# Start-up of an attention and gated-MLP kernel: all of k loaded first, the squares of k and q on two engines, norm columns earlier, and own banks for the half-width first weight products

## The chip, the cores and the metric

The kernel runs on one core of a Trainium2 chip. The metric is the device time of one execution in microseconds (us), as a median of several executions. TensorE (PE) does the matmuls, VectorE (DVE) and ScalarE (ACT) the elementwise work, GpSimd (POOL) issues the loads, SyncE (SP) the stores and the transposing loads of v. The profile is of one execution and covers a span some 1.9 us shorter than the device time. Its granted clock is the share of the full TensorE clock that PE was given.

## The reference, cut to what matters

```python
# q, k, v: (4, 6016, 256) float32; tau = 1
qn = q / (norm(q, axis=1) + 1e-6)        # norms run over the 6016 rows
kn = k / (norm(k, axis=1) + 1e-6)
s = kn.transpose(0, 2, 1) @ qn / tau     # 256 x 256 per batch
a = softmax(s, axis=-1)
x = (v @ a).reshape(24064, 256)
g = x @ w_gate                           # 256 x 1536
out = (g * sigmoid(g) * (x @ w_val)) @ w_out
```

The kernel never forms x. For each batch it multiplies the softmax matrix into both weights, once, and then multiplies v by these products. The work of batches 1 to 3 ahead of their weights runs in the background of the batch before. Batch 0 has no such cover: its loads, norms, softmax and first weight products are the start-up, and only that is changed here.

## The kernel before

The norms of batch 0 are sums of squares. An engine squares a pair of 128-row slices into `sq`; PE adds the rows up with a matrix of ones. For q the last group of slices (three of them; the other groups have four) goes straight into columns, since q's norm is wanted per partition:

```python
def first_last_q(b, ts):
    sqs = [first_square(b, t, 0, on_dve=(t == NP - 1)) for t in ts]
    row = work.tile([1, C], FP32, tag="row")
    nc.vector.tensor_copy(row, state[b, "ss", 0][0:1, :])
    for t in ts:
        gemm1_pair(b, t)
    cols = psum_gv.tile([P, CH], FP32, tag="g")
    for h in range(CH):
        nc.tensor.matmul(cols[:, h:h + 1], row[0:1, h * P:(h + 1) * P], ones_f[0:1, 0:1], ...)
    for t, sq in zip(ts, sqs):
        ...                                  # column sums of the last squares
```

Loads and squares: k three groups ahead of q; all of k's squares on VectorE, all of q's but the last pair on ScalarE.

```python
K_AHEAD = 3
for g in range(NG + K_AHEAD):
    if g < NG: order.append((g, 1))          # k
    if g >= K_AHEAD: order.append((g - K_AHEAD, 0))   # q
for n, (g, which) in enumerate(order):
    load_qk(0, g, which)
    ...
load_first_v(); load_w(0); load_v(*allc[1]); load_w(1); load_w(2)
# then w_out
```

The first weight products ("units": unit 0 and 1 are w_gate, 2 and 3 w_val, each for one half of the output rows) are made in two half widths. The lower half is all that the first two gate and value products want. Both halves share one buffer of the accumulation memory (PSUM), called a bank in what follows; to evacuate it is to copy the result out, scaled:

```python
units = [psum_gv.tile([P, WP], FP32, tag="gv"[u % 2]) for u in range(4)]
...                                          # lower halves of units 0 to 3
for u in range(4):
    wp_evacuate(b, u, units[u], lo)          # even units ScalarE, odd ones VectorE
nc.scalar.preload_act_table(ACT.Silu)
for u in range(4):
    for jh in range(CH):
        wp_matmul(b, u, jh, units[u], hi)
    wp_evacuate(b, u, units[u], hi, on_dve=True)
```

Then step f = 0 to 11 of chunk 0: a gate and a value product (`g_ps`, `v_ps`), Silu on ScalarE, the multiplication on VectorE (`sv`), and two more units in full width as long as there are any.

## Time and profile before

| | kernel before |
|---|---|
| device time, median | 821.44 us |
| span of the profile | 819.5 us |
| PE busy | 804.1 us, 98% |
| last q tile landed | 34.26 us |
| root of the norm columns begins | 36.63 us |
| units 2 and 3 (w_val) begin | 38.71 us |
| first gate product begins | 40.67 us |

The last four lines date the start-up's hand-overs, in us from the start of the span. The landing is from the trace's landing records; the others are start times in the timeline. The root is ScalarE's square root of the norm columns. From 39.65 us to the end PE has next to no gaps (3.0 us in all, in six places), so an earlier first gate product with the same work behind it is an earlier end.

### The profile page before, as it was taken

The page shows a single profiled execution, that of the slowest core. Times are in us where ns is not written, and L with a number is a line of the kernel's source. Part 1 is how long each engine was busy: PE and PEld are TensorE (multiplying, and loading weights), DVE is VectorE, ACT ScalarE, POOL GpSimd, SP SyncE. Part 2 cuts the span into 40 slices and gives each one's busy share as a digit, 9 for nine tenths or more (in the row PEclk, how much of TensorE's full clock was granted, in tenths as well). Part 3 has the DMA queues.
Part 4 walks back from the last instruction along what each step waited for, and adds up shares of the span by engine and source line. Part 5 has one row for each costly group of instructions (what it writes and reads, how often), then busy time and mean ns, then how long its engine had stood idle before and what let it go on. Part 6 is the DMA issues. An engine that isn't in the chain of part 4 may idle for free.

```text
span 819.5 us, 13681 instructions
## 1 busy us (share of the span) xinstructions
PE 804.1 (98%) x5039; PEld 488.2 (60%) x5039; DVE 552.9 (67%) x882; ACT 462.1 (56%) x826; POOL 104.7 (13%) x204
## 2 busy tenths in 40 slices
PE   7799999999999999999999999999999999999998
PEld 4556556665565655666565655666656566566666
DVE  5577888667655888856755688875856555555554
ACT  2566677545555777745555676755454544544543
POOL 5533000114310000121330000011300000000000
PEclk9999999999999999999999999999999999999999
DMA  9999812227992121123997111232562112112101
GB/s 87 145 154 139 138 40 65 52 65 114 149 153 46 55 50 40 52 52 88 143 142 126 41 52 39 40 78 64 119 118 65 46 40 65 52 39 66 49 26 59
DMA packets 92675, 64.59 MB, mean 79 GB/s; under 512 B 52560, under 2 KB 91472, under 8 KB 91856
## 3 DMA queue, kind: packets, MB, share of 16 engines
q0 software_dynamic: 18656, 27.01, 26.0%
q1 hardware_dynamic: 73952, 36.71, 18.3%
q8 instruction: 39, 0.64, 0.3%
q14 instruction: 28, 0.23, 0.1%
HBM read 78.64 MB, written 36.70 MB: 141 GB/s over the span
## 4 chain that ended last, share of the span: by engine, by line
PE 92%; DMA 2%; DVE 2%; ACT 2%; issue 1%; POOL 1%; DVEq 0%; ACTq 0%; POOLq 0%
PE o_new L456 29%; PE v_ps L428 29%; PE g_ps L428 29%; DMA q_sb<-in_q_dram 2%; PE ps L397 2%; PE kq_new L149 2%; DVE sv L432 1%; ACT sq L274 1%; DVE acc_new L283 1%; POOL k_sb L104 0%; PE ss_new L176 0%; ACT sq L166 0%; ACT silu L431 0%; PE unit_ps L397 0%; POOL q_sb L104 0%
## 5 line engine op out<-in xcount | busy, mean ns | idle before, releaser
L432 DVE TENSOR_TENSOR sv<-silu,v_ps 128x512 bf16<-128x512 bf16 (+1 forms) x576 | 382.6, 673 | 219.3 <-ACT silu L431 217.8
L431 ACT ACTIVATE silu<-g_ps 128x512 bf16<-128x512 f32 (+1 forms) x576 | 337.5, 587 | 302.0 <-PE g_ps L428 282.1
L456 PE MATMUL o_new<-w_out_sb,sv 128*128 128x256 bf16 x2256 | 338.4, 273 | 0.0
L428 PE MATMUL v_ps<-vT,Wv 128*128 128x512 bf16 (+1 forms) x1128 | 330.4, 374 | 3.0 <-DVE sv L432 3.0
L428 PE MATMUL g_ps<-vT,Wg 128*128 128x512 bf16 (+1 forms) x1128 | 331.1, 375 | 0.0
L456 PEld LDWEIGHTS <-sv 128*128 128x128 bf16 x2256 | 220.7, 98 | 140.8
L428 PEld LDWEIGHTS <-Wv 128*128 128x128 bf16 x1152 | 112.7, 98 | 135.0 <-issue 5.3
L428 PEld LDWEIGHTS <-Wg 128*128 128x128 bf16 x1152 | 106.8, 98 | 27.2 <-issue 0.2
L283 DVE TENSOR_TENSOR acc_new<-acc_new,sq 128x512 f32<-128x512 f32 x135 | 93.2, 691 | 22.1 <-ACT sq L274 19.6
L274 ACT ACTIVATE sq<-q_sb 128x512 bf16<-128x512 fp8e5 x72 | 44.3, 615 | 0.0
L274 ACT ACTIVATE sq<-k_sb 128x512 bf16<-128x512 fp8e5 x72 | 44.1, 612 | 0.0
L149 PE MATMUL kq_new<-k_sb,q_sb 128*128 128x512 fp8e5 x184 | 43.4, 318 | 0.3 <-DMA q_sb<-in_q_dram 0.3
L292 POOL CAST hi<-acc_new 128x512 bf16<-128x512 f32 x3 | 1.8, 605 | 294.3 <-DVE acc_new L283 294.3
L465 ACT COPY o_sb<-o_new 128x512 f32<-128x512 f32 x48 | 28.1, 585 | 13.6 <-PE o_new L456 12.9
L467 DVE COPY o_sb<-o_new 128x512 f32<-128x512 f32 (+1 forms) x48 | 31.7, 661 | 3.0 <-PE o_new L456 3.0
L104 POOL DMA_DIRECT2D k_sb<-in_k_dram x48 | 25.9, 542 | 38.5 <-DMA q_sb<-in_q_dram 17.7
L104 POOL DMA_DIRECT2D q_sb<-in_q_dram x48 | 26.2, 546 | 33.2 <-DMA vb<-in_v_dram 9.8
L112 POOL DMA_DIRECT2D vb<-in_v_dram x47 | 23.8, 509 | 21.2 <-DMA k_sb<-in_k_dram 16.8
L176 PE MATMUL ss_new<-sq,ones_bf 128*128 128x256 bf16 x91 | 18.6, 293 | 6.5 <-DVE sq L163 5.1
L163 DVE TENSOR_TENSOR sq<-k_sb 128x512 bf16<-128x512 fp8e5 (+1 forms) x24 | 15.3, 681 | 13.8 <-DMA k_sb<-in_k_dram 13.7
L149 PEld LDWEIGHTS <-q_sb 128*128 128x256 fp8e5 x184 | 23.1, 140 | 2.0 <-DMA q_sb<-in_q_dram 0.8
L166 ACT ACTIVATE sq<-q_sb 128x512 bf16<-128x512 fp8e5 x23 | 13.0, 619 | 19.7 <-DMA q_sb<-in_q_dram 11.9
(92 smaller groups left out, 184.9 us busy)
## 6 DMA issues: line engine op xcount, KB each, us to landing
out_dram<-o_sb SPq DMA_DIRECT2D x92, 256.0 KB, 2.4
vb<-in_v_dram POOLq DMA_DIRECT2D x43, 256.0 KB, 9.6
k_sb<-in_k_dram POOLq DMA_DIRECT2D x44, 128.0 KB, 11.4
q_sb<-in_q_dram POOLq DMA_DIRECT2D x44, 128.0 KB, 11.4
w_gate_sb<-in_moe_w_gate_dram POOLq DMA_DIRECT2D x3, 256.0 KB, 9.5
w_val_sb<-in_moe_w_val_dram POOLq DMA_DIRECT2D x3, 256.0 KB, 9.6
w_out_sb<-in_moe_w_out_dram POOLq DMA_DIRECT2D x1, 768.0 KB, 14.3
vb<-in_v_dram POOLq DMA_DIRECT2D x4, 192.0 KB, 3.4
```

The costliest lines, as they stand in the source:

```text
L104: nc.gpsimd.dma_start(out=dst[:, gs:gs + gm, :], in_=src[b].rearrange("(p s) c -> p s c", s=NS)[:, gs:gs + gm, :])
L112: nc.gpsimd.dma_start(out=vb[:mv, :].rearrange("(p s) c -> p (s c)", s=cm), in_=v[b, cs * P:cs * P + mv, :].rearrange("(p s) c -> p (s c)" ...
L149: nc.tensor.matmul(kq[:, jh, :], q_sb[:, ps:ps + 2, js], k_sb[:, ps:ps + 2, :], start=(t == 0 and jh == 0), stop=last, perf_mode=DR, skip_ ...
L176: nc.tensor.matmul(state[b, "ss", which], ones_bf, sq[:, s, :], start=(t == 0 and s == 0), stop=(t == t_last and s == pm - 1))
L274: nc.scalar.activation(sq[:, :pm, which, :], qk_tiles[b][which][:, ps:ps + pm, :], ACT.Square)
L283: nc.vector.tensor_add(acc, acc, sq[:, s, :, :])
L428: nc.tensor.matmul(dst[:, :mv], W[:, kk, fs], vT[:, kk, :mv], start=(kk == 0), stop=(kk == CH - 1))
L431: nc.scalar.activation(silu[:, :mv], g_ps[:, :mv], ACT.Silu)
L432: nc.vector.tensor_mul(sv[:, f, :mv], silu[:, :mv], v_ps[:, :mv])
L456: nc.tensor.matmul(self.o_ps[:, j % 2, :], self.sv[:, f, j * P:(j + 1) * P], w_out_sb[:, f, :], start=(f == 0), stop=(f == FH - 1))
L465: nc.scalar.copy(o_sb[:, :m, :], self.o_ps[:, :m, :])
L467: nc.vector.tensor_copy(o_sb[:, :m, :], self.o_ps[:, :m, :])
```

## The change

Its intent: get k's norm out of the way before q is done, keep either engine from falling behind with q's squares, leave next to nothing between the last q tile and the root, and take the wait for the evacuations out of the first weight products by giving their upper halves banks of their own (from the pool `psum_o`). The core of the diff:

```diff
-    K_AHEAD = 3
-    order = []
...
+    order = [(g, 1) for g in range(NG)] + [(g, 0) for g in range(NG)]
...
-    keep_warm(10)
-    T_COLS = groups[NG - 1][0] // 2
+    G_COLS = NG - 3
+    T_COLS = groups[G_COLS][0] // 2
     for g, which in order:
...
+        if which == 0 and g == G_COLS:
+            first_row_copy(0)
+        sqs = [first_square(0, t, which, on_dve=(t % 2 == 1)) for t in ts]
+        if which == 0:
+            for t in ts:
                 gemm1_pair(0, t)
+            if g == G_COLS:
+                first_cols(0)
...                                # k's norm at q group 0, its reciprocals in four
...                                # pieces of 64 columns at q groups 1 to 4
-            unit_ps = psum_gv.tile([P, WP], FP32, tag="gv"[u % 2])
+            unit_ps = psum_gv.tile([P, HW], FP32, tag="gv"[u % 2])
...
         for u in range(4):
-            wp_evacuate(b, u, units[u], lo)
+            wp_evacuate(b, u, units[u], lo, u % 2 == 1)
+        for u in range(2):
+            wp_unit(b, u, psum_o, "o", hi)
         nc.scalar.preload_act_table(ACT.Silu)
-        for u in range(4):
-            for jh in range(CH):
-                wp_matmul(b, u, jh, units[u], hi)
-            wp_evacuate(b, u, units[u], hi, on_dve=True)
...
+            g_ps, v_ps, mv = gv_matmuls(b, ci, f)
+            us = range(2 * f + 2, min(2 * f + 4, len(wp_units))) if gi == 0 else ()
+            part = hi if f == 0 else full
+            for u in us[:1]:
+                wp_unit(0, u, psum_o, "o", part, on_dve=True)
+            silu = gv_silu(g_ps, mv)
+            for u in us[1:]:
+                wp_unit(0, u, psum_o, "o", part, on_dve=(f == 0))
+            gv_product(f, sv, silu, v_ps, mv)
```

The number of matmuls for the weights is the same; the upper halves of units 2 and 3 move behind the first gate and value products.

More of the change, by code (lines that the diff above doesn't have):

```diff
@@ L177, in first_row_sums, with first_row_copy, first_cols @@
                              start=(t == 0 and s == 0), stop=(t == t_last and s == pm - 1))
-    def first_last_q(b, ts):
-        sqs = [first_square(b, t, 0, on_dve=(t == NP - 1)) for t in ts]
+    def first_row_copy(b):
         row = work.tile([1, C], FP32, tag="row")
         nc.vector.tensor_copy(row, state[b, "ss", 0][0:1, :])
-        for t in ts:
-            gemm1_pair(b, t)
+        state[b, "row"] = row
+    def first_cols(b):
+        row = state[b, "row"]
         cols = psum_gv.tile([P, CH], FP32, tag="g")
@@ L190, in first_last_q, with first_col_sums @@
                              skip_group_check=True)
-        for t, sq in zip(ts, sqs):
-            pm = pairs[t][1]
-            for s in range(pm):
-                for h in range(CH):
-                    nc.tensor.matmul(cols[:, h:h + 1], sq[:, s, h * P:(h + 1) * P],
-                                     ones_bf[:, 0:1], start=False,
-                                     stop=(t == ts[-1] and s == pm - 1),
-                                     skip_group_check=True)
-        state[b, "cols"] = cols
+        state[b, "cols"] = cols
+    def first_col_sums(b, t, sq):
+        cols = state[b, "cols"]
+        pm = pairs[t][1]
+        for s in range(pm):
+            for h in range(CH):
+                nc.tensor.matmul(cols[:, h:h + 1], sq[:, s, h * P:(h + 1) * P],
+                                 ones_bf[:, 0:1], start=False,
+                                 stop=(t == NP - 1 and s == pm - 1),
+                                 skip_group_check=True)
     def first_root(dst, src):
@@ L209, in first_norm_k, with first_inv_k @@
         state[b, "ink"] = ink
-    def first_inv_k(b, h):
-        part = state[b, "ink"][:, h * P:(h + 1) * P]
+    def first_inv_k(b, n):
+        part = state[b, "ink"][:, n * (C // 4):(n + 1) * (C // 4)]
         nc.vector.reciprocal(part, part)
@@ L235, in first_softmax @@
                                  scale=inq[:, jh:jh + 1])
-        units = []
-        for u in range(2 * CH):
-            unit_ps = psum_gv.tile([P, WP], FP32, tag="gv"[u % 2])
-            units.append(unit_ps)
         def row_sum(jh):
@@ L247, in row_sum @@
                                  stop=(jh == CH - 1), skip_group_check=True)
-        HW = WP // 2
-        lo, hi = slice(0, HW), slice(HW, WP)
+        units = []
+        for u in range(2 * CH):
+            unit_ps = psum_gv.tile([P, HW], FP32, tag="gv"[u % 2])
+            units.append(unit_ps)
         row_sum(0)
@@ L392, with wp_matmul, wp_evacuate @@
     wp_units = [(wc, w, ih) for wc in range(NWC) for w in range(2) for ih in range(CH)]
-    def wp_matmul(b, u, jh, ps, part=slice(0, WP)):
+    HW = WP // 2
+    full, lo, hi = slice(0, WP), slice(0, HW), slice(HW, WP)
+    def wp_matmul(b, u, jh, ps, part):
         wc, w, ih = wp_units[u]
         cols = slice(wc * WP + part.start, wc * WP + part.stop)
-        nc.tensor.matmul(ps[:, part], state[b, "exT"][:, jh, ih * P:(ih + 1) * P],
+        nc.tensor.matmul(ps, state[b, "exT"][:, jh, ih * P:(ih + 1) * P],
                          (w_gate_sb, w_val_sb)[w][:, jh, cols],
-                         start=(jh == 0), stop=(jh == CH - 1), skip_group_check=True)
-    def wp_evacuate(b, u, ps, part=slice(0, WP), on_dve=False):
+                         start=(jh == 0), stop=(jh == CH - 1))
+    def wp_evacuate(b, u, ps, part, on_dve):
         wc, w, ih = wp_units[u]
@@ L405, in wp_evacuate, with wp_unit, gv_matmuls @@
         dst = state[b, "W"][w][:, ih, cols]
-        if u % 2 == 0 and not on_dve:
-            nc.scalar.activation(dst, ps[:, part], ACT.Copy, scale=scale)
-        else:
-            nc.vector.tensor_scalar_mul(dst, in0=ps[:, part], scalar1=scale)
-    def wp_unit(b, u, pool=psum_m, tag="misc"):
-        ps = pool.tile([P, WP], FP32, tag=tag)
+        if on_dve:
+            nc.vector.tensor_scalar_mul(dst, in0=ps, scalar1=scale)
+        else:
+            nc.scalar.activation(dst, ps, ACT.Copy, scale=scale)
+    def wp_unit(b, u, pool=psum_m, tag="misc", part=full, on_dve=None):
+        ps = pool.tile([P, part.stop - part.start], FP32, tag=tag)
         for jh in range(CH):
-            wp_matmul(b, u, jh, ps)
-        wp_evacuate(b, u, ps)
-    def gv_step(b, ci, f, sv):
+            wp_matmul(b, u, jh, ps, part)
+        wp_evacuate(b, u, ps, part, u % 2 == 1 if on_dve is None else on_dve)
+    def gv_matmuls(b, ci, f):
         cs, cm = chunks[ci]
@@ L429, in gv_step, with gv_silu, gv_product @@
                                  start=(kk == 0), stop=(kk == CH - 1))
+        return g_ps, v_ps, mv
+    def gv_silu(g_ps, mv):
         silu = silupool.tile([P, CS * P], BF16, tag="silu")
         nc.scalar.activation(silu[:, :mv], g_ps[:, :mv], ACT.Silu)
+        return silu
+    def gv_product(f, sv, silu, v_ps, mv):
         nc.vector.tensor_mul(sv[:, f, :mv], silu[:, :mv], v_ps[:, :mv])
@@ L510 @@
     NG = len(groups)
-    K_AHEAD = 3
-    order = []
-    for g in range(NG + K_AHEAD):
-        if g < NG:
-            order.append((g, 1))
-        if g >= K_AHEAD:
-            order.append((g - K_AHEAD, 0))
+    order = [(g, 1) for g in range(NG)] + [(g, 0) for g in range(NG)]
     for n, (g, which) in enumerate(order):
@@ L534 @@
         ts = range(gs // 2, (gs + gm + 1) // 2)
-        if which == 0 and g == NG - 1:
-            first_last_q(0, ts)
-            continue
-        for t in ts:
-            if which == 0:
-                gemm1_pair(0, t)
-            first_row_sums(0, t, which, first_square(0, t, which, on_dve=(which == 1)),
-                           (T_COLS if which == 0 else NP) - 1)
+        if which == 0 and g == G_COLS:
[3 more added lines that the diff above has]
+            for t in ts:
+                gemm1_pair(0, t)
+            if g == G_COLS:
+                first_cols(0)
+        for t, sq in zip(ts, sqs):
+            if which == 0 and g >= G_COLS:
+                first_col_sums(0, t, sq)
+            else:
+                first_row_sums(0, t, which, sq, (T_COLS if which == 0 else NP) - 1)
         if which == 0:
-            after_k = g - (NG - 1 - K_AHEAD)
-            if after_k == 0:
+            if g == 0:
                 first_norm_k(0)
                 nc.vector.tensor_copy(ident, identf)
-            elif 1 <= after_k <= CH:
-                first_inv_k(0, after_k - 1)
+            elif g <= 4:
+                first_inv_k(0, g - 1)
     first_softmax(0)
-    NFIRST = 2 * CH
     prev = None
@@ L557 @@
         for f in range(FH):
-            gv_step(b, ci, f, sv)
-            if gi == 0:
-                for u in range(NFIRST + 2 * f, min(NFIRST + 2 * f + 2, len(wp_units))):
-                    wp_unit(0, u, psum_o, "o")
+            g_ps, v_ps, mv = gv_matmuls(b, ci, f)
[7 more added lines that the diff above has]
+            gv_product(f, sv, silu, v_ps, mv)
             if prev is not None:
```

## The prediction

> **What bounds the kernel now.** I read the page first. Part 1 puts TensorE at 98% of an 819.5 us span, the slices show it at 9 in all but the first two and the last, and the chain of work that ended last is 92% PE.
>
> ```profile
> PE 804.1 (98%) x5039; PEld 488.2 (60%) x5039; DVE 552.9 (67%) x882; ACT 462.1 (56%) x826; POOL 104.7 (13%) x204
> PE   7799999999999999999999999999999999999998
> PE 92%; DMA 2%; DVE 2%; ACT 2%; issue 1%; POOL 1%; DVEq 0%; ACTq 0%; POOLq 0%
> ```
>
> The reader is to see that the body is one unbroken run of matmuls, so that only its start and the work inside it count. The diff leaves that work alone: 16 half products of the first weights, 16 full ones, and the same gate, value and output matmuls. Everything it touches comes before some 50 us. So the question is how much earlier the unbroken run of PE starts.
>
> Next I read the timeline of the first 60 us. Columns: start, us, engine, line, operation, tiles, count, idle time before and what ended it.
>
> ```profile
> 34.83 0.35 DVE L163 TENSOR_TENSOR sq<-q_sb 128x256 bf16<-128x256 fp8e5 x1
> 35.29 0.41 DVE L183 COPY row<-ss_new 1x256 f32<-1x256 f32 x1
> 35.76 0.60 PE L188 MATMUL cols<-ones_f,row 1*128 1x1 f32 x4
> 36.29 0.30 PE L195 MATMUL cols<-ones_bf,sq 128*128 128x1 bf16 x6
> 36.63 0.17 ACT L202 ACTIVATE inq<-cols 128x2 f32<-128x2 f32 x1 [1.29 <-PE cols L195]
> ...
> 38.71 0.60 PE L397 MATMUL unit_ps<-w_val_sb,exT 128*128 128x256 bf16 x4
> 39.65 0.60 PE L397 MATMUL unit_ps<-w_gate_sb,exT 128*128 128x256 bf16 x4 [0.34 <-ACT Wg L407]
> 40.67 0.59 PE L428 MATMUL g_ps<-vT_new,Wg 128*128 128x512 bf16 x2
> ```
>
> Two serial stretches are there. After the last q tile: its squares, the copy of the row, four small and six tiny matmuls, then the root. And at the first weights: the upper halves (39.65) must wait until ScalarE has emptied the lower halves of the same buffers, since PE is done with the lower ones at about 39.1. From 39.65 PE never stops.
>
> Last, the queue. GpSimd issues a load only when an earlier one has landed, so its idle times date the landings.
>
> ```profile
> 35.77 1.05 POOL L529 DMA_DIRECT2D w_out_sb<-in_moe_w_out_dram  x1 [0.53 <-DMA v_sb<-in_v_dram]
> 37.05 0.52 POOL L112 DMA_DIRECT2D vb<-in_v_dram  x1 [0.23 <-DMA w_gate_sb<-in_moe_w_gate_dram]
> 38.38 0.57 POOL L104 DMA_DIRECT2D q_sb<-in_q_dram  x1 [0.81 <-DMA w_val_sb<-in_moe_w_val_dram]
> ```
>
> Each issue follows the landing by 0.28 us (in the trace's own landing records: last q 34.26, v 35.49, w_gate 36.77, w_val 38.10). Landings come every 1.25 us from 5.18 on, and the windows view has the DMA engines full from 4 us. So the first w_val slice, 27th in the queue, lands at 38.10 whatever the engines do. In the kernel before it is wanted at 38.71: only 0.6 us of slack.
>
> **What the skill says.** The page "DMA: Bandwidth & Descriptors", section "Bandwidth", gives a fabric ceiling of 435 GB/s and 425 measured. A q or k tile lands as 128 KB of fp8 but is read as 512 KB of float32, every 1.25 us: 419 GB/s. It agrees, so the order of the loads cannot change when the last one lands. The page "TensorE: Matmul & The Clock Gate", Part 1, says the clock is halved after an idle window of about 3.4 us and full again after a busy one. The trace agrees: the ten warm-up matmuls start 0.43 us apart, the same shape goes every 0.216 us later, and the windows view shows a granted clock of 0.50 from 11 to 14 us, after a stretch in which only two row sums of 0.11 us came every 0.6 us. "PSUM — Partial Sum Buffer", section "PSUM bank collisions raise a hardware error", tells to guard a buffer by bank, which is why the upper halves wait for the evacuation; the 39.65 line agrees. "ScalarE: Activation LUTs", section "What ACT_TABLE_LOAD costs", has about 1283 ns, and the trace's load of the Silu table took 1.28 us.
>
> **The change, part by part.**
>
> (1) Loads: all of k, then all of q, in place of k three groups ahead. Same 24 loads, same bytes, same rate: the last q still lands at 34.26. Worth 0 by itself.
>
> (2) Squares on both engines. Before, ScalarE squared all of q but the last pair (0.58 us a pair, 1.15 a group against 1.25 between landings) and fell behind when it also took the two activations for k's norm (0.36 and 0.42 us at 31.9): five squares ran from 32.65 to 35.34 without a gap. Now a group costs one square of 0.6 on each engine, so the last q squares end at 34.26 + 0.04 + 0.62 = 34.92 in place of 35.34. The k norm falls to the first q group, 12 us earlier; its reciprocals, 1.75 us in two pieces, become four pieces, off the path.
>
> (3) Columns from the third last group on. The row copy (0.41) and its four matmuls (0.60) move two groups earlier. After the last square only the tiny column sums remain: 34.92 + 0.04 + about 0.30 + 0.04 = 35.30 for the root, against 36.63. That is 1.33 us.
>
> (4) From the root to units 2 and 3 the chain is unchanged (36.63 to 38.71, 2.08 us with seven hand-overs). It would put them at 37.4. But their w_val lands at 38.10; PE sees a landing within 0.05 us. So they start at 38.15, and 0.8 of the 1.33 us is lost to the load. v (35.49, for its transposes) and w_gate (36.77, wanted at about 36.75) do not bind.
>
> (5) Own banks. Behind units 2 and 3 (four half products) the upper halves of units 0 and 1 follow in another pool without a wait, then the first gate matmul: 38.15 + 8 x 0.1075 = 39.01. Before, that matmul came at 40.67, with 16 half products done and 12 now; the four postponed ones cost 4 x 0.1075 = 0.43 later. The gain is 40.67 - (39.01 + 0.43) = 1.23 us. As a check: 0.56 from the earlier start (38.71 to 38.15), 0.5 from the wait for ScalarE (about 39.14 to 39.65), and 0.16 at 40.5, where the first gate product waited for a VectorE evacuation.
>
> (6) Evacuations and the order in the first steps. ScalarE: lower half of unit 2 until about 39.0, upper of unit 0 until 39.5, table load 1.28 until 40.8, Silu until 41.4. VectorE multiplies until 42.1; PE wants that value buffer at about 42.5. Gate product 2 needs Silu 0 (41.4) and comes at 42.05. Unit 6 needs unit 4's buffer, emptied at about 42.85, and comes at 42.9. All just fit; per step with two units VectorE has 0.69 + 0.75 = 1.44 us against PE's 1.73. Cost 0 to 0.1.
>
> (7) No ten warm-up matmuls: they ran while PE waited for k; cost 0 unless the clock suffers (below).
>
> Sum: 0.56 + 0.5 + 0.16 = about 1.2 us, less up to 0.1: 821.44 - 1.15 = 820.3.
>
> **Rivals.** (A) *The w_val load does not bind*, because loads land earlier in runs without the profiler or the q7 load (2.1 us after its forerunner in this trace, not 1.25) has no such hiccup. Then the whole of the 1.33 us counts and the sum is 1.33 + 0.66 = 2.0: 819.4. Against it: the queue is full from 4 us on. (B) *The clock.* While k alone is loaded PE has four row sums of 0.21 us (cold) every 1.25 us, or 34% when warm, the density at which the clock was taken away at 10.8 us. PE may enter q cold. There a group costs about 1.75 us cold (0.88 a pair at 11 to 12 us) and 1.04 warm, against 1.25 between landings. Cold for two windows (6.8 us) makes a lag of 6.8 x (1 - 1.25/1.75) = 1.9 us, of which six or seven warm groups win back 0.21 each: some 0.6 us left, which still fits in the 0.8 that the load hides. If more is left, or if the wait for w_val brings a cold window at 38 us, the gain goes: up to 3.4 us at half speed costs 1.7, 821.9. (C) *The table load* becomes the bound: if the upper half of unit 0 reaches ScalarE late, Silu 0 slips past 41.8 and PE stalls for some tenths: 820.7. (D) *Nothing*: the body takes the gain back at a later load. The chunk 1 and 2 transposes landed at 48.4 and 68.1, wanted at 54.5 and about 70, and the weight slices about 1 us or more ahead of use; PE coming 1.2 us sooner still finds them there. 821.3.
>
> **Range and chances.** Main line 820.3; A pulls to 819.4, C and D to 820.7 to 821.3, B beyond. Runs of the kernel before spread over 0.6 us. So 819.3 to 821.3 should hold it 8 times in 10. 2% is 16.4 us: all of PE's idle time in the first 40 us that this could touch is less than that, and no rival costs so much. Chances: faster 0.005, same 0.99, slower 0.005.
>
> **What would show it.** In the changed profile: last q landing near 34.3; the root of the columns at 35.2 to 35.5; units 2 and 3 waiting for the w_val load and starting at 38.1 to 38.2, with 0.6 to 0.9 us of PE idle before; no PE wait for ScalarE or VectorE between there and the first gate product at about 39.0; PE unbroken from 38.15. Wrong if the column root comes after 36, if the granted clock is under 1 after 35 us, or if units 2 and 3 start well before 38 (rival A).

## The result, and the profile after

The changed kernel takes 820.0 us (median of 5 runs, 819.79 to 820.49) against 821.44 (821.2 to 822.04): 1.44 us or 0.2% less (far from the 2% that would count as faster), with a ratio of 0.9982 (95% interval 0.9968 to 0.9997). Ratios are the mean time of one kernel's runs over the mean of the other's of the same rounds, so not quite the ratio of the medians quoted.

Part 1 of the page of the changed kernel (engine, busy us, share, instructions):

```profile
PE 801.7 (98%) x5037; PEld 487.7 (60%) x5037; DVE 552.7 (68%) x882; ACT 464.5 (57%) x828; POOL 104.8 (13%) x204
```

The body is as it was. In both kernels the only waits of PE after 60 us are six for the multiplication on VectorE, 3.0 us in all. So the 1.4 us of span (819.5 to 818.1) must lie in the start-up. A rival is the clock: in the profile before it was halved from 10.65 to 14.07 us (mean 0.998), in the one after its mean is 1.000. That did not bring the gain: of the nine runs of the kernel before in the last round, the four with a mean of 1.0 took 821.05 to 821.39 us, the five others 821.23 to 821.65. The timeline of the changed kernel there, the lines that answer to those of the prediction:

```profile
34.19 0.63 ACT L166 ACTIVATE sq<-q_sb 128x512 bf16<-128x512 fp8e5 x1 [0.29 <-DMA q_sb<-in_q_dram]
...
34.87 0.30 PE L199 MATMUL cols<-ones_bf,sq 128*128 128x1 bf16 x6
35.21 0.17 ACT L205 ACTIVATE inq<-cols 128x2 f32<-128x2 f32 x1 [0.39 <-PE cols L199]
...
37.98 0.61 PE L398 MATMUL unit_ps<-w_val_sb,exT 128*128 128x256 bf16 x4 [0.52 <-DMA w_val_sb<-in_moe_w_val_dram]
38.22 0.57 POOL L104 DMA_DIRECT2D q_sb<-in_q_dram  x1 [0.81 <-DMA w_val_sb<-in_moe_w_val_dram]
...
38.42 0.60 PE L398 MATMUL ps<-w_gate_sb,exT 128*128 128x256 bf16 x4
...
38.86 0.59 PE L429 MATMUL g_ps<-vT_new,Wg 128*128 128x512 bf16 x2
...
39.29 0.59 PE L429 MATMUL v_ps<-vT_new,Wv 128*128 128x512 bf16 x2
39.33 1.28 ACT L265 ACT_TABLE_LOAD   x1
```

The row copy and its matmuls are gone from the end of q; the root starts 1.42 us earlier (36.63 to 35.21). But units 2 and 3 start only 0.73 us earlier (38.71 to 37.98), and their line says why: PE waited for the load of w_val. Behind them nothing waits. The first gate product comes 1.81 us earlier (40.67 to 38.86) with four half products, 0.43 us, still owed: 1.38 us, the whole of the gain in span.

The chain that ended last, of the changed kernel (start, us, what; cut here to 18 to 39 us), shows the new bound at once:

```profile
18.03 9.44 DMA q_sb<-in_q_dram
27.47 0.28 issue
27.75 10.18 DMA w_val_sb<-in_moe_w_val_dram
37.93 0.04 issue
37.98 0.61 PE unit_ps L398 x4
38.59 0.44 PE ps L398 x4
39.02 0.43 PE g_ps L429 x2
```

No square, root or softmax is on it any more. Before the change it ran through all of these; now it is the issue of the loads and their queue up to 37.93 us, then PE.

### The profile page after: what moved, and what is told of

It reads as the page before. It is cut to its first block, busy times and chain, and to the rows that moved or that the text cites. A ratio compares the mean times of both kernels' runs of the same rounds, so it can differ in the third digit from the quotient of the medians.

```text
span 818.1 us, 13674 instructions
## 1 busy us (share of the span) xinstructions
PE 801.7 (98%) x5037; PEld 487.7 (60%) x5037; DVE 552.7 (68%) x882; ACT 464.5 (57%) x828; POOL 104.8 (13%) x204
## 4 chain that ended last, share of the span: by engine, by line
PE 92%; DMA 4%; DVE 1%; ACT 1%; issue 1%; POOL 1%; DVEq 0%; ACTq 0%; POOLq 0%
PE o_new L463 29%; PE v_ps L429 29%; PE g_ps L429 29%; PE ps L398 2%; PE kq_new L149 2%; DMA w_val_sb<-in_moe_w_val_dram 1%; DMA k_sb<-in_k_dram 1%; DMA q_sb<-in_q_dram 1%; ACT sq L272 1%; DVE sv L439 1%; POOL k_sb L104 1%; DVE acc_new L281 1%; ACT silu L435 0%; PE ps L331 0%; PE cs L305 0%
## 5 line engine op out<-in xcount | busy, mean ns | idle before, releaser
L272 ACT ACTIVATE sq<-q_sb 128x512 bf16<-128x512 fp8e5 x72 | 44.2, 614 | 0.0
L149 PE MATMUL kq_new<-k_sb,q_sb 128*128 128x512 fp8e5 x184 | 40.5, 313 | 0.5 <-DMA q_sb<-in_q_dram 0.5
L104 POOL DMA_DIRECT2D k_sb<-in_k_dram x48 | 25.8, 546 | 37.1 <-DMA q_sb<-in_q_dram 20.1
L176 PEld LDWEIGHTS <-ones_bf 128*128 128x128 bf16 x83 | 9.9, 124 | 15.5 <-issue 11.2
L163 DVE TENSOR_TENSOR sq<-k_sb 128x512 bf16<-128x512 fp8e5 (+1 forms) x12 | 8.0, 670 | 9.6 <-DMA k_sb<-in_k_dram 6.1
```

Of the source, the lines that this page charges most:

```text
L104: nc.gpsimd.dma_start(out=dst[:, gs:gs + gm, :], in_=src[b].rearrange("(p s) c -> p s c", s=NS)[:, gs:gs + gm, :])
L149: nc.tensor.matmul(kq[:, jh, :], q_sb[:, ps:ps + 2, js], k_sb[:, ps:ps + 2, :], start=(t == 0 and jh == 0), stop=last, perf_mode=DR, skip_ ...
L176: nc.tensor.matmul(state[b, "ss", which], ones_bf, sq[:, s, :], start=(t == 0 and s == 0), stop=(t == t_last and s == pm - 1))
L272: nc.scalar.activation(sq[:, :pm, which, :], qk_tiles[b][which][:, ps:ps + pm, :], ACT.Square)
```

## The experiments

My theory: the start-up is bounded by the load queue as soon as the chain behind q is short enough; units 2 and 3 cannot begin before w_val has landed. Rivals: the chain from the norm's root still sets them; and, for the split of the gain, that the parts of the change simply add up in the sizes of the prediction (0.73 us for loads, squares and columns, 0.66 for own banks). There were twelve runs, two of them repeats, in three rounds with five executions each; each round has nine executions of the kernel before beside them. All gave correct results.

| run | median us | lowest to highest | ratio to before |
|---|---|---|---|
| first half of the change alone | 820.13 | 820.08 to 820.19 | 0.9984 |
| second half alone | 821.01 | 820.75 to 821.52 | 0.9997 |
| change, weights one load later | 821.25 | 820.94 to 823.8 | 1.0004 |
| change, first weight slices in halves | 819.67 | 819.36 to 820.24 | 0.9980 |
| same, v of chunk 1 later | 826.81 | 825.26 to 827.02 | 1.0064 |
| change, columns from the last group | 820.27 | 819.97 to 820.79 | 0.9988 |
| slices in halves, columns from the last group | 820.06 | 819.9 to 820.13 | 0.9985 |
| first half alone, slices in halves | 820.39 | 820.19 to 820.45 | 0.9989 |
| change, loads in the old order | 821.18 | 820.59 to 821.56 | 0.9996 |
| weights one load later, more fillers | 821.31 | 820.87 to 821.56 | 0.9999 |
| the change again | 820.13 | 819.96 to 820.62 | 0.9987 |
| slices in halves again | 819.5 | 819.43 to 819.7 | 0.9977 |

The median of before was 821.27, 821.3 and 821.38 in the three rounds (four lines each).

### Is it the load? Weights one load later

```diff
-    load_w(0)
     load_v(*allc[1])
+    load_w(0)
```

> The changed kernel with the v rows of chunk 1 queued ahead of the first weight slices, which so land one load later. My theory, that the w_val load sets the start of the unbroken run: units 2 and 3 start 1.3 to 1.6 us later, at 39.2 to 39.5, and the time rises by the same, to 821.3 to 821.6. Rival, the chain from the root sets it and the load is only just in time: less than 1.0 us.

```profile
37.94 0.39 PE L398 MATMUL unit_ps<-w_gate_sb,exT 128*128 128x256 bf16 x2 [1.08 <-DMA w_gate_sb<-in_moe_w_gate_dram]
...
39.20 0.61 PE L398 MATMUL unit_ps<-w_val_sb,exT 128*128 128x256 bf16 x4 [0.60 <-DMA w_val_sb<-in_moe_w_val_dram]
```

PE now waits for both slices. w_val landed at 39.15 and units 2 and 3 started at 39.20, which is 1.22 us after the change's 37.98. The three quick runs were 820.94, 821.13 and 821.25: about 1.1 us above the change (820.0; its repeat had 820.13). So a delay of the load arrives in the time nearly whole, though somewhat less than the forecast 1.3 us. The time alone is close to the rival's limit of 1.0 us; it is the wait for the landing in the profile that makes the rival fall. Two runs were slower still, 822.84 and 823.8. Both have a mean granted clock of 0.998, the three quick ones 1.0. The profile is of the first of these, and the windows of it from 35 to 39 and 39 to 43 us show a cause (columns: window, length, busy us and count of PE, PEld, DVE, ACT, POOL, then granted clock, DMA share, GB/s):

```profile
35.00:39.00 4.00, 2.34 (x25) 1.26 (x25) 2.09 (x9) 1.43 (x5) 2.25 (x4) 1.00 1.16 193
39.00:43.00 4.00, 3.81 (x17) 2.22 (x18) 1.57 (x4) 3.15 (x5) 1.58 (x3) 0.60 1.23 200
```

PE was busy for 2.34 of 4 us while it waited for the weights, and right after that its clock was halved (from 39.77 to 43.18 us). Half speed for 3.4 us would cost 1.7 us, an estimate that fits the 822.84; a further 1.0 us of the 823.8 stays open. Whether the thin work of PE is the cause of the slow runs was tried with more fillers, matmuls whose result nobody reads:

```diff
-        keep_warm(3)
+        keep_warm(10)
```

> The third experiment again (weights one load later) with ten filler matmuls behind the transposes of v in place of three; they end at about 38.0, where PE stands still for the w_gate load anyway. In the third experiment the profile has the clock halved from about 39.6 to 43, and two of five runs were 822.8 and 823.8 against 820.9 to 821.3. My theory: PE's idle time of over 2 us ahead of 39.2 let the clock down in some runs; with the fillers the clock stays at 1.00, all five runs lie within 820.9 to 821.5. Rival: the slow runs have another cause: the spread stays.

```profile
35.00:39.00 4.00, 3.57 (x32) 2.05 (x32) 2.04 (x8) 1.28 (x5) 2.40 (x4) 1.00 1.15 192
39.00:43.00 4.00, 3.64 (x23) 2.26 (x24) 2.68 (x7) 3.66 (x6) 1.59 (x3) 1.00 1.22 198
```

With PE busy for 3.57 of the 4 us the clock stayed at 1.00, and the five runs lay within 820.87 to 821.56 with no slow ones. Five runs are few, so this is good evidence rather than proof. In the changed kernel itself the wait is shorter, and none of its ten runs was above 820.62.

### Take the load away: the first slices in halves

```diff
-    def load_w(wc):
-        cols = slice(wc * WP, (wc + 1) * WP)
+    def load_w(wc, part=slice(0, 512)):
+        cols = slice(wc * WP + part.start, wc * WP + part.stop)
...
-    load_w(0)
+    load_w(0, lo)
+    load_w(0, hi)
```

> The changed kernel with the first slices of both weights loaded in two halves, the lower halves of w_gate and w_val first. The w_val half that units 2 and 3 need then lands at about 36.6. My theory: the chain takes over, units 2 and 3 start at about 37.3, first gate matmul at about 38.2 (it must wait for the evacuations of units 0 and 1), the Silu table load then costs 0.1 to 0.3 us: gain over the changed kernel 0.35 to 0.65 us, 819.4 to 819.7. Rival, smaller loads are slower and all weights land later: no gain. Rival, the load was not what units 2 and 3 waited for: no gain.

The lower half of w_val landed at 36.53 us. PE in the timeline:

```profile
37.11 0.60 PE L398 MATMUL unit_ps<-w_val_sb,exT 128*128 128x256 bf16 x4
37.55 0.60 PE L398 MATMUL ps<-w_gate_sb,exT 128*128 128x256 bf16 x4
38.05 0.61 PE L429 MATMUL g_ps<-vT_new,Wg 128*128 128x512 bf16 x2
...
40.42 0.82 PE L398 MATMUL ps<-w_gate_sb,exT 128*128 128x512 bf16 x3
```

Units 2 and 3 no longer wait and start 0.87 us earlier than in the changed kernel. So the load did hold them, and the chain alone would have let them start at about 37.1 to 37.3. Not all of it stays: the second gate slice landed at 40.38, and unit 4 wanted it at 40.23, so 0.19 us went there; the cost expected from the table load did not appear. The next load in the queue is at once the next bound.

For a fair comparison this kernel and the change ran once more in the same rounds:

> The changed kernel itself, as the measure for the others of these rounds: 819.8 to 820.5, 1.1 to 1.5 us under the kernel before.

> The kernel of the fourth experiment beside the changed kernel in the same rounds. In the fourth experiment its first gate matmul came 0.8 us earlier than in the changed kernel and 0.19 us went at unit 4, its span was 0.5 us shorter. My theory: 0.3 to 0.6 us faster than the change. Rival: run-to-run differences of the loads' landing are as large, no difference seen.

The medians are 819.5 and 820.13. The slowest of the five runs in halves (819.7) is below the quickest of the change (819.96); in the first round the runs in halves had spread from 819.36 to 820.24, so it is the repeat that decides. So this version beats both kernels: 0.6 us under the change and 1.9 us under the kernel before (821.38). The second profile of the change also tells how much the loads scatter: w_val landed at 38.11 in place of 37.93, and the span was 818.3 in place of 818.1.

The stall at unit 4 invited one more step, to put the second slices ahead of the v rows of chunk 1:

```diff
-    load_v(*allc[1])
     load_w(1)
+    load_v(*allc[1])
     load_w(2)
```

> The changed kernel with the first slices in halves as in the fourth experiment, and the v rows of chunk 1 moved behind the second slices of both weights. In the fourth experiment PE stood still for 0.19 us at unit 4, which wanted the second w_gate slice (landed 40.38). My theory: that slice now lands at about 39.1, the stall goes: 0.1 to 0.2 us faster than the fourth experiment, about 819.5. Rival: the transposed v of chunk 1 then comes too late for its first use at about 52.8 (it took 9 us from its rows' landing in the changed kernel) and PE waits: slower by 0.5 or more.

The rival was right, and at a far higher price than the stall:

```profile
57.14 1.03 PE L429 MATMUL g_ps<-vT,Wg 128*128 128x512 bf16 x2 [4.43 <-DMA vT<-vb]
```

Unit 4's wait did go (it started at 40.35, right behind the value product). But the transposing load of chunk 1's v was issued at 41.81 and landed only at 57.10, 15.3 us later; in the changed kernel it was issued at 39.56 and landed at 48.73, 9.2 us later (in the kernel in halves, issued at 39.15 and landed at 48.19). A delay of 2.25 us at its issue became 8.4 us at its landing, and PE stood still for 4.43 us. After that stop its clock was halved (0.55 from 56 to 60 us), which adds to the loss of 7 us.

### Which part brought the gain?

The first half alone keeps the order of loads, the squares and the columns of the change, and has the weight products as before; the second half alone is the reverse.

```diff
 # first half alone, against the changed kernel
-        for u in range(2):
-            wp_unit(b, u, psum_o, "o", hi)
         nc.scalar.preload_act_table(ACT.Silu)
+        for u in range(4):
+            for jh in range(CH):
+                wp_matmul(b, u, jh, units[u], hi)
+            wp_evacuate(b, u, units[u], hi, on_dve=True)
 # ... and the full-width buffers and step order of before
```

> Only the first half of the change: all of k first, squares on both engines, columns from the third last group; the first weight products as in the kernel before (upper halves in the same buffers). My theory: units 2 and 3 still wait for the w_val load and start at about 38.0; that wait gives ScalarE and VectorE time to empty the lower halves of units 0 and 1, so the upper halves wait little; the first gate matmul comes at about 39.65 (40.67 before; 38.86 with four half products still owed in the changed kernel). Time 820.4, gain 1.0 us. Rival, the two halves of the change add up (0.56 + 0.17 from this half, 0.66 from the other): gain 0.75, 820.7. Rival, the load is not the bound: units 2 and 3 start at 37.4.

> Only the second half: upper halves of units 0 and 1 in their own pool, those of 2 and 3 after the first gate and value products, new order of evacuations; loads, squares and columns as in the kernel before. My theory: units 2 and 3 start at 38.7 as before, no wait for ScalarE behind them, first gate matmul at about 39.57 with four halves owed: gain 0.66 us, 820.8. Rival, the load of the Silu table (later than before in ScalarE's order) stalls PE at the third value product: gain 0.2 to 0.4.

The first half alone gives 1.14 us (821.27 to 820.13), close to all of the gain. Its timeline:

```profile
37.90 0.61 PE L400 MATMUL unit_ps<-w_val_sb,exT 128*128 128x256 bf16 x4 [0.51 <-DMA w_val_sb<-in_moe_w_val_dram]
38.35 0.60 PE L400 MATMUL unit_ps<-w_gate_sb,exT 128*128 128x256 bf16 x4
38.86 0.61 PE L400 MATMUL unit_ps<-w_val_sb,exT 128*128 128x256 bf16 x4
39.48 0.59 PE L431 MATMUL g_ps<-vT_new,Wg 128*128 128x512 bf16 x2
```

While PE waits for w_val, ScalarE and VectorE empty the lower halves of units 0 and 1, so the upper halves follow at 38.35 without a wait for them although the buffer is shared. Own banks save here about 0.27 us: the first gate product comes 1.58 us after the start of units 2 and 3 with all half products done, against 0.88 us with 0.43 us owed. So the sizes of the prediction, 0.73 us for this half and 0.66 for the other, do not hold: the wait for one thing hides the wait for another.

The second half alone measured 0.26 us (821.27 to 821.01, ratio 0.9997, interval 0.9984 to 1.0009), which is not clear of zero and under the 0.66 expected. Its profile has units 2 and 3 at 38.55 and the first gate product at 39.50, so the wait for ScalarE is gone there; a later one of 0.12 us appears at unit 6, which wants the buffer of unit 4. The rival was right in size (0.2 to 0.4 us) and partly in mechanism: Silu starts at 41.48, when the table load ends, VectorE multiplies from 42.11 and empties unit 4 only from 42.72 to 43.47, and unit 6 starts at 43.52. The stall, though, is at that unit and not at the third value product. The runs scatter over 0.8 us, and how much of the rest was lost to what stays open. That the two measured gains, 1.14 and 0.26, come to 1.40 tells nothing, since the interval of the second is 2 us wide.

If the shared banks are hidden by the load, they should come back when the load is taken away:

```diff
 # first half alone
-    load_w(0)
+    load_w(0, slice(0, 256))
+    load_w(0, slice(256, 512))
```

> The first half of the change alone, as in the first experiment, with the first weight slices loaded in halves. My theory: units 2 and 3 start at 37.1, then the upper halves wait for the evacuations of the lower ones (first gate matmul at about 39.05 with all 16 half products done, against 38.05 with four owed, 0.43 us, in the fourth experiment): about 0.4 us slower than the fourth experiment, so that own banks are worth most when the load does not bind. Rival, own banks bring nothing here either: same as the fourth experiment within 0.15 us.

```profile
37.30 0.60 PE L400 MATMUL unit_ps<-w_val_sb,exT 128*128 128x256 bf16 x4
38.25 0.60 PE L400 MATMUL unit_ps<-w_gate_sb,exT 128*128 128x256 bf16 x4 [0.34 <-ACT Wg L410]
...
40.61 1.04 PE L400 MATMUL ps<-w_gate_sb,exT 128*128 128x512 bf16 x4 [0.32 <-DMA w_gate_sb<-in_moe_w_gate_dram]
```

They do: the wait for ScalarE is back at 38.25. At 820.39 this kernel is 0.7 to 0.9 us slower than its counterpart with own banks (819.67, and 819.5 in the repeat), more than the 0.4 expected. By the time lines 0.60 of it lies before the first gate product, which comes 1.97 us after the start of units 2 and 3 with all half products done, against 0.94 us with 0.43 us owed; another 0.13 lies at the second gate slice, which stops this kernel for 0.32 and its counterpart for 0.19. It isn't even quicker than the same half with whole slices (820.13, in another round). So own banks are worth 0.3 us at most with the load in the way and 0.7 to 0.9 without it.

### The columns from the third last group on

```diff
-    G_COLS = NG - 3
+    G_COLS = NG - 1
```

> The changed kernel with the columns only from the last group on, as before the change (row copy and its four matmuls after the last q tile). My theory: the root comes about 0.6 us later (35.8 against 35.21), which the wait for w_val hides: units 2 and 3 still start at 38.0, time within 0.15 us of the changed kernel, 820.0 to 820.15. Rival, the earlier columns are what brought the gain: 0.5 us or more slower.

> The same edit on the fourth experiment's kernel, where the load no longer binds. My theory: here the 0.6 us count, less the 0.19 us stall at unit 4 which the later start absorbs: 0.3 to 0.6 us slower than the fourth experiment, about 820.1. Rival, the columns are hidden here too: 0.

On the change: 820.27 against 820.0 and 820.13 in the other rounds, a little above the 820.15 forecast and inside the scatter of both. All loads came early in this profile (w_val at 37.62), and units 2 and 3 started at 37.81, 4.02 us after the last q tile (33.79); with early columns and slices in halves it was 3.21 us (33.90 to 37.11). The late columns thus cost 0.8 us of chain (0.7 in the kernel in halves: 33.97 to 37.89, 3.92 us), where I had expected 0.6, and nearly all of that is hidden by w_val, which lands 3.8 us after the last q. On the kernel in halves, where nothing hides it: 820.06 against 819.67 and 819.5, 0.4 to 0.6 us slower, as expected.

### The order of the loads

The old order needs k's norm later, so it and its four reciprocals go back to the last groups of q:

```diff
-    order = [(g, 1) for g in range(NG)] + [(g, 0) for g in range(NG)]
+    ...                       # k three groups ahead of q, as in the kernel before
...
-            if g == 0:
+            after_k = g - (NG - 1 - K_AHEAD)
+            if after_k == 0:
                 first_norm_k(0)
                 nc.vector.tensor_copy(ident, identf)
-            elif g <= 4:
-                first_inv_k(0, g - 1)
+            elif 1 <= after_k <= 2:
+                first_inv_k(0, 2 * after_k - 2)
+                first_inv_k(0, 2 * after_k - 1)
```

> The changed kernel with the loads in the old order (k three groups ahead of q), so that k's norm and its reciprocals fall to the last four q groups again; squares on both engines, early columns and own banks stay. My theory, step 1 of the prediction: the order of the loads is worth nothing by itself. The last q lands 3.8 us before w_val as ever, the root of the columns comes 1.1 to 1.4 us after the last q (1.12 in the changed kernel), units 2 and 3 wait for w_val: within 0.15 us of the change in the same rounds. Rival: without k first the norm of k delays the last squares by more than the 0.62 us that the load hides: 0.3 us or more slower.

My theory failed here and the rival held: 821.18 against 820.13 for the change in the same rounds, so almost the whole gain is lost. The last q (34.10) and w_val (37.94) landed as ever. From its timeline:

```profile
34.24 0.62 DVE L163 TENSOR_TENSOR sq<-q_sb 128x512 bf16<-128x512 fp8e5 x1
34.79 0.94 DVE L216 RECIPROCAL ink<-ink 128x64 f32<-128x64 f32 x2
...
35.65 0.35 DVE L163 TENSOR_TENSOR sq<-q_sb 128x256 bf16<-128x256 fp8e5 x1
...
36.31 0.17 ACT L205 ACTIVATE inq<-cols 128x2 f32<-128x2 f32 x1 [1.48 <-PE cols L199]
...
39.03 0.60 PE L398 MATMUL unit_ps<-w_val_sb,exT 128*128 128x256 bf16 x4
```

VectorE now has half of q's squares and also the reciprocals, in order. The last square waits behind 0.94 us of them and starts at 35.65, although its data had landed at 34.10. The root comes at 36.31, 2.2 us after the last q in place of 1.1; these 1.1 us are more than the 0.6 to 0.7 that the load hides. In addition the windows view of this profile has a granted clock of 0.52 from 36 to 39 us (two filler matmuls took 1.06 us there):

```profile
36.00:39.00 3.00, 2.72 (x20) 1.98 (x22) 1.67 (x8) 1.28 (x4) 1.75 (x3) 0.52 1.15 208
```

In the runs the two with a mean granted clock of 1.0 took 820.59 and 820.63, the three with 0.998 took 821.18 to 821.56. By that reading the reciprocals cost about 0.5 us and the halved window another 0.8 in three of five runs; the split rests on five runs only.

## Why the prediction was right

The predicted 820.3 (819.3 to 821.3) held 820.0. By its own steps:

- **Which bound.** Right: the w_val load took over. The chain of the changed kernel shows it, the run with weights one load later moved the start of units 2 and 3 by 1.22 us and the time by about 1.1, and the run with half slices moved the start of units 2 and 3 forward by 0.87.
- **(1) Loads worth 0 by itself.** Right for what it said of the landings, wrong as a value for the part. With the old order and all else changed the gain is nearly gone (821.18). The step that failed is that I credited the early k norm to the squares as "off the path", and not to the order of loads that makes it possible. Where VectorE takes half of q's squares, its reciprocals must not stand in front of the last ones.
- **(2), (3) Squares and columns.** The root came 1.12 us after the last q landed, 1.04 was predicted. Two of the three parts of this were tested: late columns cost 0.7 to 0.8 us of chain, nearly all hidden; the late k norm costs 1.1, of which some 0.5 shows. The squares on two engines were not tried alone.
- **(4) The hidden share.** Predicted 0.8 us. With the root at 35.21 and the unchanged 2.08 us behind it, units 2 and 3 could have started at 37.29 and started at 37.98: 0.69. Of the signs named, the start (38.1 to 38.2) and PE's idle time before it (0.6 to 0.9) came out lower, at 37.98 and 0.52; in the second profile of the same kernel they were 38.15 and 0.51. The kernel in halves confirms it: its units 2 and 3, which nothing held, began 3.21 us after the last q landed, and 1.12 + 2.08 is 3.20.
- **(5) Own banks.** The first gate product came 0.88 us after units 2 and 3 began, 0.86 was predicted. But the account of 0.5 + 0.16 us for this part was false as an attribution: the first half alone, without own banks, already has 1.14 of the 1.44 us. The wait for the load had taken the place of the wait for ScalarE. Read as a sum the prediction held only because it counted from one kernel's time line to the other's and not part by part.
- **(6) Evacuations.** Silu 0 ran at 40.63 (40.8 predicted), and PE had no stall; the 0.05 us set aside were not needed.
- **(7) and rival B, the clock.** In this profile PE did run cold through all of k: four row sums took 1.01 us each time until 20 us, and 0.61 or less from 23.75 on. (The trace's clock record begins at 23.05, with the full clock; the windows view's 1.00 for the time before is no reading.) It caught up: the last products of k and q start at 34.17, at once after the last landing. In the second profile of the same kernel the full clock came at 14.43, in the middle of k:

```profile
13.46 1.01 PE L176 MATMUL ss_new<-sq,ones_bf 128*128 128x256 bf16 x4 [0.24 <-ACT sq L166]
14.76 0.60 PE L176 MATMUL ss_new<-sq,ones_bf 128*128 128x256 bf16 x4 [0.29 <-ACT sq L166]
```

So a cold start into q comes and goes between executions of the same kernel, and as it was caught up it cost nothing that shows: the profile that was cold for longer has the shorter span (818.1 against 818.3). A slip in rival B: 820.3 + 1.7 is 822.0, not 821.9. That the ten warm-up matmuls cost nothing was not tried alone.

- **The size.** 1.15 predicted, 1.44 measured, 1.4 in the span. Of the difference, 0.15 to 0.17 us are loads that landed earlier in this profile (w_val at 37.93, not 38.10), and the rest is the reserve of step 6 and scatter. In the second profile of the same kernel w_val landed at 38.11, and the gain in those rounds was 1.25 us.

## What to carry to other kernels

Before shortening a chain, date the landings of everything it will want next: here 0.7 of 1.4 us stopped at a load that had 0.6 us of slack before, and loading just the half that was wanted first gave back some 0.6 us in the same rounds. What a part of a start-up is worth depends on the others: own banks brought 0.3 us at most behind the load and 0.7 to 0.9 without it. So test a part alone and everything but that part, since one wait can hide another. When work is moved to a second engine, look at what else that engine does in the last microsecond before the result is wanted.

## What the Trainium skill lacked or had wrong

- "TensorE: Matmul & The Clock Gate", Part 1, names an idle window of about 3.4 us, and short pauses, as what takes the clock away, but gives no measure of how busy a window must be. In the kernel before the clock fell at 10.65 us although no pause of PE since it came at 7.24 was longer than 0.49 us; with the weights one load later it fell at 39.77, with PE busy for 2.34 of the 4 us up to 39, in several pieces; with 3.57 of 4 us busy it stayed. On the way up, four row sums of 1.01 us every 1.25 us brought the full clock at 14.43 us in one profile of the changed kernel and not before 23.05, when the products of q had joined them, in the other.
- "ScalarE: Activation LUTs", section "What ACT_TABLE_LOAD costs", adds about 1380 ns of drain to the 1283 ns of a table load. In the changed kernel the evacuation before the load ended at 39.31, the load ran from 39.33 for 1.28 us and Silu began at 40.63, 0.02 us after its end; no drain shows on either side.
- None of the pages I read gives a time for a transposing load that shares the DMA engines with a full queue of GpSimd's loads. Against the kernel in halves, with the second weight slices ahead of it, it was issued 2.66 us later (41.81, not 39.15) and landed 8.91 us later (57.10, not 48.19).
